# Two token tiles multiplied together, 512 columns wide, in a windowed-attention and two-layer kernel

## The chip, the cores and the metric

The kernel runs on one core of one Trainium2 chip. The metric is the device time of one execution in microseconds; the median of three runs before the change is 878.5 us (878.42 to 878.53).

## What is computed

Attention with a window of 128 keys and a linear position bias, then two feed-forward layers on its 2304 token rows (4 batches of 576, 8 heads of 64, so 512 features). Layer 1 is the one that the change works on.

```python
scores = scale * (q @ k.T) + slope * -abs(rel)      # masked to 0 <= rel < 128
x = softmax(scores) @ v                              # (2304, 512)
h = x @ moe_w_in;   g = h * clip(h + 3, 0, 6) / 6;   x = g @ moe_w_out        # 512 -> 2048 -> 512
h = x @ moe2_w_in;  g = s * relu(h)**2 + b;          out = g @ moe2_w_out
```

All weights come as float64 (two 32-bit words an element).

## The kernel before, in words

**Tiles.** Layer 1 cuts the 2304 token rows into eight tiles: tiles 0 to 3 have 256 rows (the first two query blocks of each batch), tiles 4 to 7 have 320. Its weights are 16 blocks of 128 hidden features; block `f` holds an input half (512 features by 128) and an output half (128 by 512). A `Step(t, f)` is one block for one tile: `h` (L939) multiplies 12 times into the one PSUM bank of tag `h`; `relu` (ScalarE, L950) reads that bank; `product` (VectorE, L953) reads it a last time and so frees it; `hi` (ScalarE, L960) and `lo` (VectorE, L964) split the result in two float32r parts; `o` (L977) multiplies 12 times into four accumulators. A number is split in a high and a low part everywhere, and three of the four products of parts are taken, hence 3 x 4 matmuls a group. After block 15, `end` (L990 to L995) scales the accumulators and stores the tile to DRAM.

**Weights.** Each float64 block is converted on the chip in two halves (`Half`, L319 on): `high` (ScalarE, L355) rescales the upper words into a staging buffer `staging_early`; a second ScalarE operation (L361) rescales the lower words; `sign` (VectorE, a shift L371 and an or L374, or one operation L366 for the halves in `SIGN_ON_POOL`, whose sign bit GpSimd has cut out at L358); `add` (GpSimd, L380); `hi` (ScalarE, L386); `lo` (VectorE, L390; GpSimd for four halves). All 32 halves are converted while tiles 0 and 1 are worked on.

**Order.** There is no scheduler at run time: each method is put in a numbered slot with a rank (`at`), a table `MOVED` shifts single ones, and the sorted list is the order in which every engine's queue is filled. A pair of slots is one `Step`. The first slots hold the attention of tile 0 and 1 (`StartUnit`) and warming matmuls (`FILLERS`). Steps of tile 0 come first; tile 1 follows three blocks behind (`LAG = 3`), alternating with tile 0. From tile 2 on a tile is done at a stretch, with the attention of the tile after it in between. A half's slots follow from its number:

```python
s = 4 * f + 2 * i if f > 4 else min(s - 6, 3 + 4 * f + 2 * i)
```

**Second layer.** Its weights are converted too (`Pair`, 16 of them, during tiles 2 to 7), written to DRAM through a staging buffer and the raw buffers (`target`, L1120), and read back as 1 MB chunks into a ring of five buffers (`Chunk`, L1161) when the second layer runs (L1410, L1344).

Of the kernel before, what the change touches and what calls it, by code (L numbers as in the profile page):

```python
# [12 lines left out]
I32 = mybir.dt.int32  # L13
# [13 lines left out]
COPIED_ON_VECTOR = ("0_0_2", "1_0_2", "1_0_6")  # L27

SIGN_ON_POOL = ("0_1", "4_0", "6_0")

HALF_SHIFTS = {
    "0_0": 2, "0_1": 1, "10_0": 1, "10_1": 1, "2_1": -1, "3_0": 1, "3_1": 1, "4_1": 2, "5_1": 1,
    "8_0": 1, "8_1": 1, "9_1": 1,
}

FILLERS = (3, 1, 0, 0, 0, 2, 2, 1, 2, 1, 0, 2, 0, 0)

KINDS = {"StartUnit": "S", "MidUnit": "M", "Unit": "U", "Step": "T", "Half": "H", "Pair": "P", "Rest": "R"}


def names(fn):
# [6 lines left out]
    if c is None:  # L48
        return ()
    m = method.__name__ + ("." + str(args[0]) if args else "")  # L50
    own = f"{o.t}_{o.f}" if c == "T" else str(o.i) if c == "P" else o.id
    kind = {
        "S": lambda: f"{o.g}{o.h % 2}", "M": lambda: o.h % 2, "U": lambda: o.h % 2, "R": lambda: "",
# [9 lines left out]
    "Ha0.load": (1, 0),  # L63
    "Ha1.high": (0, 2.05),
    "Ha1.lo": (0, -1.6),
# [21 lines left out]
    "S10.widen": (-1, 0),  # L87
# [24 lines left out]
    "M2_0_0.load_values": (2, 0),  # L112
    "M2_0_2.load_values": (-1, 0),
    "M2_0_3.to_lo": (-1, 0),
    "M2_0_4.exps": (-2, 0),
    "M2_0_5.weights": (2, 0.3),
    "M2_0_7.minima": (2, -1.92),
    "S01.to_lo": (1, -7.4),
# [8 lines left out]
    "S1_0_0.scale": (1, 0),  # L127
    "S1_0_2.exps": (1, -3.2),
# [11 lines left out]
    "T1_6.product": (0, -0.05),  # L140
}
# [3 lines left out]
def tile_alibi_window_attention_moe_moe2(  # L145
# [22 lines left out]
    N1 = max(SIZES1)  # L168
    N2 = 384
# [59 lines left out]
    own = const.tile([P, P], I32, name="own")  # L229
# [40 lines left out]
    def half_blocks():  # L270
        nonlocal own2, relp, slope
        own2 = ap.tile([P, HALF], I32, bufs=1, name="own2")
        relp = ap.tile([P, P], F32, bufs=1, name="relp")
        slope = ap.tile([P, H // 2], F32, bufs=1, name="slope")
        for i in (0, 1):
            p = slice(i * HALF, (i + 1) * HALF)
            nc.sync.dma_start(out=relp[p], in_=rel[:HALF])
            nc.sync.dma_start(out=own2[p], in_=own[:HALF, :HALF])
            for j in range(H // 2):
                nc.gpsimd.memset(slope[p, j : j + 1], slopes[2 * j + i])  # L280

# [36 lines left out]
    class Half:  # L318
# [29 lines left out]
        def high(self):  # L348


            if "early" not in late:
                late["early"] = ap.tile([P, 4 * DM], F32, tag="stage", bufs=1, name="staging_early")
# [559 lines left out]
    class Step:  # L912
# [17 lines left out]

        def h(self):
            w = wt[self.f]
            x = x_tile(self.t)
# [3 lines left out]
            for cc in range(CC):  # L937
                for wp, xp in ((0, 0), (0, 1), (1, 0)):
                    nc.tensor.matmul(  # L939
                        self.ps,  # L940
                        lhsT=w[:, wp, cc * P : (cc + 1) * P],
                        rhs=x[:, cc, xp],
# [5 lines left out]
        def relu(self):  # L948
            self.a = gpool.tile([P, N1], F32, tag="t", name=f"t{self.t}_{self.f}")[:, : self.n]
# [7 lines left out]
        def hi(self):  # L957
            self.g = gpool.tile([P, 2, N1], F32R, tag="g", name=f"g{self.t}_{self.f}")
# [6 lines left out]

        def o(self):
            t, f = self.t, self.f
            if f == 0:
                ids = ((0, 1), (2, 3))[t] if t < 2 else range(CC)
                acc[t] = [ps_o.tile([P, 512], F32, tag=f"o{d}", name=f"o{t}_{d}") for d in ids]  # L970
                if t < 2:
                    acc[t] = [a[:, i : i + 256] for a in acc[t] for i in (0, 256)]
                acc[t] = [a[:, : self.n] for a in acc[t]]
            w = wt[f]
            for i, (wp, gp) in enumerate(((0, 0), (1, 0), (0, 1))):
                for d in range(CC):
                    nc.tensor.matmul(  # L977
                        acc[t][d],
                        lhsT=w[:, wp, DM + d * P : DM + (d + 1) * P],
                        rhs=self.g[:, gp],  # L980
                        start=f == 0 and i == 0 and (t > 1 or d % 2 == 0),
# [3 lines left out]

        def end(self):
            t, n = self.t, self.n
            for e in range(0, CC, 2):
                y = gpool.tile([P, 2, N1], F32, tag="y", name=f"y{t}_{e}")[:, :, :n]
                nc.scalar.activation(y[:, 0], acc[t][e], AF.Copy, scale=1.0 / 6.0)  # L990
# [633 lines left out]
```

## Time and profile before

| | before |
|---|---|
| median of three runs | 878.5 us |
| the profiled execution, its own time | 878.33 us |
| its span, first to last instruction | 876.6 us |
| TensorE, VectorE, ScalarE, GpSimd busy | 99%, 72%, 59%, 39% of the span |
| mean granted TensorE clock | 0.998 of full speed |
| first `h` group; first `h` group of tile 2 | 29.24 us; 146.62 us |

TensorE's line shows when one of its instructions was in work; a row of the timeline gives start, length and, in brackets, the idle time before it with the instruction that ended it. Two rows that follow each other overlap a little, so the time that a group takes is read from one start to the next. In the shapes, `128x256` is partitions by columns.

### The profile page before, as it was taken

The numbers are of one execution on the slowest core, as the hardware profiler recorded it, in microseconds if no ns is written. First come the engines' busy times: TensorE is split into PE (matmuls) and PEld (weight loads), VectorE is DVE, ScalarE is ACT, GpSimd is POOL, SyncE is SP. The second block draws the span as 40 slices with busy tenths as digits, with TensorE's granted clock in tenths as the row PEclk, the third lists the DMA queues.
The fourth block names the chain that finished last, engine by engine and source line by source line (L and its number), as shares of the span: only waits on it lengthen the run. The fifth ranks groups of instructions, "written<-read, shape, count | busy, mean of one in ns | idle before, by whom it ended". The sixth has DMA issues, their size and how long they took to land.

```text
span 876.6 us, 17097 instructions
## 1 busy us (share of the span) xinstructions
PE 866.7 (99%) x6154; PEld 817.2 (93%) x6156; DVE 630.0 (72%) x1391; ACT 516.4 (59%) x1196; POOL 339.5 (39%) x539
## 2 busy tenths in 40 slices
PE   8999999999999999999999999999999999999998
PEld 5889899999999999999999999998899988999887
DVE  6898985566787677767657536779847789577784
ACT  7978875555665556465545436666356656366551
POOL 5644541334565454545534303453114450144200
PEclk9999999999999999999999999999999999999999
DMA  9554433526475556465555707887788787777873
GB/s 330 182 156 144 130 93 102 176 78 219 151 260 178 174 188 215 155 204 165 189 170 190 290 22 263 284 295 258 257 281 314 275 289 246 271 252 264 293 244 112
DMA packets 66821, 183.15 MB, mean 209 GB/s; under 512 B 9904, under 2 KB 29616, under 8 KB 58288
## 3 DMA queue, kind: packets, MB, share of 16 engines
q1 hardware_dynamic: 66736, 182.06, 61.4%
q8 instruction: 49, 0.80, 0.4%
q14 instruction: 36, 0.29, 0.1%
HBM read 143.13 MB, written 38.80 MB: 208 GB/s over the span
## 4 chain that ended last, share of the span: by engine, by line
PE 95%; DVE 3%; issue 1%; ACT 1%; ACTq 0%
PE h L939 23%; PE o L977 23%; PE h L1410 20%; PE o L1344 20%; PE v L687 2%; PE s L546 1%; PE t L643 1%; PE t L809 1%; PE tv L824 1%; PE v L888 1%; DVE w L390 1%; PE s L531 1%; PE s L778 1%; PE s L566 1%; PE warm_ps L224 1%
## 5 line engine op out<-in xcount | busy, mean ns | idle before, releaser
L977 PE MATMUL o<-g,w 128*128 128x256 f32 (+1 forms) x1536 | 233.0, 301 | 0.0
L939 PE MATMUL h<-x,w 128*128 128x256 f32 (+1 forms) x1536 | 227.8, 297 | 3.3 <-DVE t L953 3.3
L977 PEld LDWEIGHTS o<-g,w 128*128 128x128 f32 x1536 | 211.4, 190 | 7.5 <-issue 3.8
L939 PEld LDWEIGHTS h<-x,w 128*128 128x128 f32 x1536 | 211.9, 190 | 5.3 <-DVE t L953 4.3
L1410 PE MATMUL h<-x,wstream 128*128 128x384 f32 x1008 | 176.8, 334 | 0.0
L1344 PE MATMUL o<-wstream,i 128*128 128x256 f32 (+1 forms) x1032 | 176.4, 332 | 0.0
L1410 PEld LDWEIGHTS h<-x,wstream 128*128 128x128 f32 x1008 | 174.4, 188 | 0.8 <-ACT s L1420 0.6
L1344 PEld LDWEIGHTS o<-wstream,i 128*128 128x128 f32 x1032 | 155.3, 188 | 19.8
L950 ACT ACTIVATE t<-h 128x256 f32<-128x256 f32 (+1 forms) x128 | 52.4, 410 | 160.3 <-PE h L939 159.3
L953 DVE SCALAR_TENSOR_TENSOR t<-t,h 128x256 f32<-128x256 f32 (+1 forms) x128 | 57.7, 450 | 87.2 <-ACT t L950 86.7
L964 DVE TENSOR_TENSOR g<-t,g 128x256 fp32r<-128x256 f32 (+1 forms) x128 | 72.6, 567 | 19.4 <-ACT g L960 18.7
L1444 ACT ACTIVATE g<-g,scalar 128x384 f32<-128x384 f32 x96 | 58.5, 610 | 39.4 <-DVE g L1429 36.9
L1467 POOL TENSOR_TENSOR g<-g 128x384 f32<-128x384 f32 x24 | 24.3, 1012 | 112.3 <-PE h L1410 93.4
L960 ACT ACTIVATE g<-t 128x256 fp32r<-128x256 f32 (+1 forms) x128 | 56.2, 439 | 12.7 <-DVE t L953 12.5
L1428 DVE TENSOR_TENSOR g<-h,s 128x384 f32<-128x384 f32 x72 | 39.8, 552 | 31.3 <-PE h L1410 22.6
L672 POOL TENSOR_SCALAR_AFFINE_SELECT W<-F 128x128 f32<-128x128 f32 (+1 forms) x128 | 38.7, 337 | 33.5 <-ACT F L647 31.5
L622 POOL TENSOR_SCALAR P<-P,st 128x128 f32<-128x128 f32 x80 | 37.4, 481 | 32.0 <-DVE st L431 30.7
L1194 DVE SCALAR_TENSOR_TENSOR i<-g,scalar,i 128x768 fp32r<-128x768 f32 x48 | 49.2, 1071 | 0.6 <-ACT i L1193 0.6
L1429 DVE SCALAR_TENSOR_TENSOR g<-g 128x384 f32<-128x384 f32 x72 | 47.3, 658 | 2.5
L1091 POOL TENSOR_TENSOR work<-raw 128x512 int32<-128x512 int32 x28 | 29.9, 1086 | 39.7 <-ACT P L605 11.7
L1420 ACT ACTIVATE s<-h 128x384 f32<-128x384 f32 x72 | 34.7, 481 | 17.8 <-PE h L1410 17.4
L1193 ACT ACTIVATE i<-g,scalar 128x768 fp32r<-128x768 f32 x48 | 41.5, 930 | 5.8 <-PE o L1344 5.8
(147 smaller groups left out, 1175.0 us busy)
## 6 DMA issues: line engine op xcount, KB each, us to landing
wstream<-wo SPq DMA_DIRECT2D x42, 1024.0 KB, 4.9
raw<-w SPq DMA_DIRECT2D x53, 512.0 KB, 5.0
wstream<-wh SPq DMA_DIRECT2D x24, 1024.0 KB, 5.7
wstream<-wh SPq DMA_DIRECT2D x24, 768.0 KB, 6.0
wh<-staging_early SPq DMA_DIRECT2D x16, 512.0 KB, 3.6
wo<-staging_early SPq DMA_DIRECT2D x12, 512.0 KB, 3.2
stage<-w SPq DMA_DIRECT2D x11, 512.0 KB, 4.4
out<-u SPq DMA_DIRECT2D x11, 384.0 KB, 3.1
```

What stands on the lines that cost most here:

```text
L939: nc.tensor.matmul(self.ps, lhsT=w[:, wp, cc * P : (cc + 1) * P], rhs=x[:, cc, xp], start=m == 0, stop=m == 3 * CC - 1,)
L950: nc.scalar.activation(self.a, self.ps, AF.Relu, bias=3.0)
L953: nc.vector.scalar_tensor_tensor(out=self.a, in0=self.a, scalar=6.0, in1=self.ps, op0=ALU.min, op1=ALU.mult)
L960: nc.scalar.activation(self.g[:, 0], self.a, AF.Copy)
L964: nc.vector.tensor_tensor(out=self.g[:, 1], in0=self.a, in1=hi, op=ALU.subtract)
L977: nc.tensor.matmul(acc[t][d], lhsT=w[:, wp, DM + d * P : DM + (d + 1) * P], rhs=self.g[:, gp], start=f == 0 and i == 0 and (t > 1 or d % 2 ...
L1193: nc.scalar.activation(hi, src, AF.Identity, bias=b)
L1194: nc.vector.scalar_tensor_tensor(out=out[:, :, 1], in0=src, scalar=b, in1=hi.bitcast(F32), op0=ALU.add, op1=ALU.subtract,)
L1344: nc.tensor.matmul(self.acc[k][c][:, out], lhsT=g[:, gp, c * P : (c + 1) * P], rhs=w[:, cols], start=k in (0, 1, 5) and p == 0 and i == 0, ...
L1410: nc.tensor.matmul(self.ps[first], lhsT=w[:, wp, cc], rhs=x[:, cc, xp], start=n == first and m == 0, stop=m == 5, skip_group_check=True,)
L1429: nc.vector.scalar_tensor_tensor(out=g, in0=g, scalar=0.0, in1=g, op0=ALU.max, op1=ALU.mult)
L1444: nc.scalar.activation(g, g, AF.Copy, scale=s_sb)
```

## The change

From block 4 on the steps of tiles 0 and 1 are one (`Both`): one `h` group of 12 matmuls with 512 columns, one `relu`, `product`, `hi` and `lo` on 512 columns, one `o` group of 12 with 512 columns. The x of the two tiles lies in one buffer `both`; a wide `h` reads it as two runs of 256. The accumulators of the two tiles are now the halves of the same four banks. Blocks 0 to 3 stay at 256 columns and run first for tile 0, then for tile 1 (`LAG = 4`). The conversion of blocks from 5 on is planned six slots later (`LATER`), the steps that need them are as much later. `staging_early` is half as large (two places for `high` instead of four), the `Pair` stores come from other buffers, and the ring of chunks uses the two halves of `both`. Five `high` go from ScalarE to GpSimd (`HIGH_ON_POOL`), five more halves have their sign cut out on GpSimd (`SIGN_ON_POOL`), four copies of attention go from ScalarE to VectorE (`COPIED_ON_VECTOR`), three warming matmuls go, and `MOVED` has other entries.

```diff
-COPIED_ON_VECTOR = ("0_0_2", "1_0_2", "1_0_6")
+COPIED_ON_VECTOR = ("0_0_0", "0_0_2", "0_0_5", "0_0_7", "1_0_0", "1_0_2", "1_0_6")
+HIGH_ON_POOL = ("3_0", "4_1", "5_1", "6_0", "7_0")
-SIGN_ON_POOL = ("0_1", "4_0", "6_0")
+SIGN_ON_POOL = ("0_1", "10_0", "11_0", "1_1", "2_0", "4_0", "6_0", "8_1")
-FILLERS = (3, 1, 0, 0, 0, 2, 2, 1, 2, 1, 0, 2, 0, 0)
+FILLERS = (2, 1, 0, 0, 0, 1, 1, 1, 2, 1, 0, 2, 0, 0)
...
     "T0.h": (0, 9),
+    "T0.o": (0, 10.3),
...
-    LAG = 3
-    steps = []
-    for i in range(NF + LAG):
-        steps += [(0, i)] if i < NF else []
-        steps += [(1, i - LAG)] if i >= LAG else []
+    LAG = 4
+    steps = [(t, f) for t in range(2) for f in range(LAG)]
+    steps += [(t, f) for f in range(LAG, NF) for t in range(2)]
     steps += [(t, f) for t in range(2, nt1) for f in range(NF)]
...
+    for f in range(LAG, NF):
+        hslot[1, f] = hslot[0, f]
+        oslot[0, f] = oslot[1, f] = hslot[0, f] + (5 if f < NF - 1 else 3)
...
-        free = 4 if slot < FIRST else 2 if slot < hslot[1, 0] else 0
+        free = 4 if slot < FIRST + 2 else 0
...
-            self.zp = late["early"][:, late["z"] % 4 * DM :][:, :DM]
-            nc.scalar.activation(self.zp, self.h.bitcast(F32), AF.Copy, scale=2.0**-112)
+            self.zp = late["early"][:, late["z"] % 2 * DM :][:, :DM]
+            h = self.h.bitcast(F32)
+            if self.id in HIGH_ON_POOL:
+                nc.gpsimd.tensor_scalar(
+                    out=self.zp, in0=h, scalar1=2.0**-112, scalar2=1.0, op0=ALU.mult, op1=ALU.mult
+                )
+            else:
+                nc.scalar.activation(self.zp, h, AF.Copy, scale=2.0**-112)
...
+    both = xpool.tile([P, 2, 2 * CC * N1], F32R, name="both")
...
+    class Both(Step):
...
+        def plan(self):
+            s = hslot[0, self.f]
+            at(s + 1, 10, self.h)
+            at(s + 2, 30.05, self.relu)
+            at(s + 2, 31.5, self.product)
+            at(s + 3, 30.05, self.hi)
+            at(s + 3, 31.7, self.lo)
+            s = oslot[0, self.f]
+            at(s + 1, 10, self.o)
+            if self.f == NF - 1:
+                at(s + 1, 30, self.end)
...
+        def values(self, cc, xp):
+            return both[:, :, (2 * cc + xp) * N1A :][:, :, :N1A]
...
-            whole = staging(self.s) if j < 2 else self.raw.bitcast(F32)
-            return whole[:, j % 2 * 2 * DM : j % 2 * 2 * DM + n * DM]
+            if j < 2:
+                whole = self.raw.bitcast(F32)[:, j * 2 * DM :]
+            elif j == 2:
+                whole = staging(self.s)
+            else:
+                whole = self.L[:, self.kind * DM :]
+            return whole[:, : n * DM]
...
-    ring = ("s0", "s1", "x1", "x2", "s2")
+    ring = ("s0", "s1", 1, "x2", 0)
...
+    LATER = 6
...
-            s = 4 * f + 2 * i if f > 4 else min(s - 6, 3 + 4 * f + 2 * i)
+            s = 4 * f + 2 * i + LATER if f > 4 else min(s - 6, 3 + 4 * f + 2 * i)
...
-    ready = (done, done, done, done, max(done, half))
+    ready = (done, done, done, done, max(done, hslot[nt1 - 1, NF - 1] + 2))
```

Three places of the new order on which the prediction rests. In the names `t`, `h`, `o` and `g` are followed by tile and block or accumulator, `w1_5` is block 5 of the weights, and the last number is a buffer's.

VectorE before, from the `product` of tile 1's block 0 to that of tile 0's block 4:

```order
L953 SCALAR_TENSOR_TENSOR t1_0_779<-t1_0_779,h1_0_766 128x256
L371 TENSOR_SCALAR staging_early_246<-staging_early_246 128x512
L374 SCALAR_TENSOR_TENSOR raw1_206<-raw1_206,staging_early_246 128x512
L964 TENSOR_TENSOR g1_0_800<-t1_0_779,g1_0_800 128x256
L390 TENSOR_TENSOR w1_5_803<-raw1_206,w1_5_803 128x512
L371 TENSOR_SCALAR staging_early_246<-staging_early_246 128x512
L374 SCALAR_TENSOR_TENSOR raw0_205<-raw0_205,staging_early_246 128x512
L953 SCALAR_TENSOR_TENSOR t0_4_824<-t0_4_824,h0_4_811 128x256
```

VectorE in the changed kernel, from the `product` of tile 1's block 3 to the first wide one:

```order
L1001 SCALAR_TENSOR_TENSOR t1_3_878<-t1_3_878,h1_3_864 128x256
L432 TENSOR_TENSOR w1_4_764<-raw1_202,w1_4_764 128x512
L432 TENSOR_TENSOR w1_5_899<-raw1_202,w1_5_899 128x512
L413 TENSOR_SCALAR staging_early_241<-staging_early_241 128x512
L416 SCALAR_TENSOR_TENSOR raw0_201<-raw0_201,staging_early_241 128x512
L1012 TENSOR_TENSOR g1_3_896<-t1_3_878,g1_3_896 128x256
L408 SCALAR_TENSOR_TENSOR stage6_0_857<-staging_early_241,stage6_0_857 128x512
L1001 SCALAR_TENSOR_TENSOR t0_4_945<-t0_4_945,h0_4_907 128x512
```

Block 5's conversion stood right behind tile 1's first step; now it stands behind tile 1's fourth, before the first wide `product`.

TensorE before, around the `h` group of block 8 for tile 0:

```order
L977 MATMUL o0_0_607<-g0_7_1113,w1_7_985 128x256 x2
L977 MATMUL o0_1_608<-g0_7_1113,w1_7_985 128x256 x2
L939 MATMUL h0_8_1181<-x0_279,w1_8_1095 128x256 x12
L977 MATMUL o1_2_834<-g1_4_1170,w1_4_720 128x256 x2
L977 MATMUL o1_3_835<-g1_4_1170,w1_4_720 128x256 x2
```

TensorE in the changed kernel, around the wide `h` group of block 5:

```order
L987 MATMUL h0_5_956<-both_96,w1_5_899 128x512 x12
L1031 MATMUL o0_0_609<-g0_4_954,w1_4_764 128x512
L1031 MATMUL o0_1_610<-g0_4_954,w1_4_764 128x512
L1031 MATMUL o0_2_611<-g0_4_954,w1_4_764 128x512
L1031 MATMUL o0_3_612<-g0_4_954,w1_4_764 128x512
```

An `h` group and an `o` group of 256 columns for each tile, each weight loaded for both tiles in turn, became one of each with 512 columns.

ScalarE before, in the start, around the copies of two transposed units (`W0_0_4`, `W0_0_5`):

```order
L386 ACTIVATE w1_0_312<-raw1_206 128x512
L698 ACTIVATE x0_279<-tv0_0_3_297 128x256
L817 ACTIVATE W0_0_4_346<-t0_0_4_293 128x384
L817 ACTIVATE W0_0_5_350<-t0_0_5_334 128x384
L800 ACTIVATE P1_0_0_342<-P1_0_0_342,st_126 128x128
```

ScalarE in the changed kernel at the same place:

```order
L428 ACTIVATE w1_0_308<-raw1_202 128x512
L741 ACTIVATE both_96<-tv0_0_3_290 128x256
L860 ACTIVATE W0_0_4_343<-t0_0_4_319 128x384
L843 ACTIVATE P1_0_0_339<-P1_0_0_339,st_133 128x128
L843 ACTIVATE P1_0_0_339<-P1_0_0_339,st_133 128x256
```

The copy of unit 5 has left ScalarE for VectorE; three others of the start did the same.

## Rows read from the trace of the kernel before

**Rows 1.** The page's busy table: engine, busy us, share of the span, instructions.

```profile
PE 866.7 (99%) x6154; PEld 817.2 (93%) x6156; DVE 630.0 (72%) x1391; ACT 516.4 (59%) x1196; POOL 339.5 (39%) x539
```

**Rows 2.** Stretches: length, busy us by engine, granted clock, DMA share, GB/s.

```profile
12.00:28.00 16.00, 14.01 (x110) 10.98 (x112) 15.37 (x51) 15.72 (x37) 10.36 (x17) 1.00 0.94 361
...
52.00:56.00 4.00, 2.16 (x13) 1.96 (x12) 3.96 (x6) 3.05 (x6) 2.10 (x3) 0.81 0.75 223
56.00:60.00 4.00, 4.00 (x29) 4.00 (x29) 3.78 (x7) 2.95 (x6) 1.91 (x2) 0.77 0.44 142
60.00:120.00 60.00, 58.51 (x479) 54.37 (x478) 55.02 (x128) 51.09 (x129) 28.21 (x31) 1.00 0.46 139
120.00:870.00 750.00, 749.97 (x5244) 713.32 (x5243) 524.35 (x1111) 415.65 (x957) 277.60 (x436) 1.00 0.63 214
```

**Rows 3.** List of waits, TensorE: us in total, times, longest.

```profile
PE h L939 <- DVE t L953: 3.3, 4, 1.8
```

**Rows 4.** Timeline of VectorE before the longest gap: start, length.

```profile
50.92 1.53 DVE L390 TENSOR_TENSOR w<-raw,w 128x512 fp32r<-128x512 f32 x1
52.37 0.41 DVE L371 TENSOR_SCALAR staging_early<-staging_early 128x512 int32<-128x512 int32 x1
...
53.75 0.41 DVE L953 SCALAR_TENSOR_TENSOR t<-t,h 128x256 f32<-128x256 f32 x1
```

**Rows 5.** Timeline of TensorE behind that gap.

```profile
54.21 2.74 PE L939 MATMUL h<-x,w 128*128 128x256 f32 x12 [1.84 <-DVE t L953]
56.75 2.08 PE L977 MATMUL o<-g,w 128*128 128x256 f32 x12
58.67 1.60 PE L939 MATMUL h<-x,w 128*128 128x256 f32 x12
60.11 1.60 PE L977 MATMUL o<-g,w 128*128 128x256 f32 x12
...
63.05 0.93 PE L531 MATMUL s<-raw 64*128 64x128 f32 x8
63.91 1.70 PE L977 MATMUL o<-g,w 128*128 128x256 f32 x12
```

**Rows 6.** Timeline of TensorE, second layer; 512 and 256 columns alternate in L1344.

```profile
583.53 56.32 PE L1344 MATMUL o<-wstream,i 128*128 128x512 f32 x324
639.69 56.33 PE L1410 MATMUL h<-x,wstream 128*128 128x384 f32 x324
695.85 1.20 PE L1344 MATMUL o<-wstream,i 128*128 128x512 f32 x6
```

**Rows 7.** Timeline of VectorE, 61 to 64 us.

```profile
61.12 0.42 DVE L371 TENSOR_SCALAR staging_early<-staging_early 128x512 int32<-128x512 int32 x1
61.58 0.69 DVE L374 SCALAR_TENSOR_TENSOR stage<-stage,staging_early 128x512 int32<-128x512 int32 x1
62.19 0.42 DVE L964 TENSOR_TENSOR g<-t,g 128x256 fp32r<-128x256 f32 x1
62.52 1.53 DVE L390 TENSOR_TENSOR w<-stage,w 128x512 fp32r<-128x512 f32 x1
63.98 0.41 DVE L953 SCALAR_TENSOR_TENSOR t<-t,h 128x256 f32<-128x256 f32 x1
...
64.86 0.68 DVE L390 TENSOR_TENSOR w<-stage,w 128x512 fp32r<-128x512 f32 x1
```

**Rows 8.** Line L817, 8 to 40 us: ns min/median/max, first and last start.

```profile
L817 ACT ACTIVATE W<-t x13: 467/485/514, 9.8 to 39.2; 128x384 f32<-128x384 f32 x13
```

**Rows 9.** The page's DMA issues: count, KB each, median us to landing.

```profile
wstream<-wh SPq DMA_DIRECT2D x24, 1024.0 KB, 5.7
```

**Rows 10.** Line L358: ns min/median/max.

```profile
L358 POOL TENSOR_SCALAR raw<-raw x2: 669/670/672, 13.1 to 41.7; 128x512 f32<-128x512 f32 x2
```

**Rows 11.** Timeline of GpSimd at 62 us.

```profile
62.41 1.10 POOL L380 TENSOR_TENSOR stage<-stage 128x512 int32<-128x512 int32 x1 [1.96 <-DVE stage L374]
```

**Rows 12.** Groups by form, VectorE, 54 to 141 us: busy us, mean ns.

```profile
L390 DVE TENSOR_TENSOR w<-raw,w 128x512 fp32r<-128x512 f32 x15 | 15.8, 1051 | 1.2 <-ACT w L386 0.9
```

More of the change, by code (lines that the diff above doesn't have):

```diff
@@ L91 @@
     "S11.transposes": (-1, 2),
+    "S11.values": (0, -2),
     "T0.h": (0, 9),
+    "T0.o": (0, 10.3),
+    "T1.lo": (0, 6.3),
     "T1.o": (0, -1),
+    "T1.product": (0, -1.42),
+    "U0.scale": (1, 6.0),
     "H0_1.hi": (-1, 0),
+    "H11_0.high": (-2, 2.05),
+    "H13_0.load": (1, 0),
+    "H14_0.add": (0, 0.6),
     "H14_0.high": (-1, 0),
@@ L226, in tile_alibi_window_attention_moe_moe2 @@
     ident = const.tile([P, P], F32, name="ident")
-    own = const.tile([P, P], I32, name="own")
+    own = const.tile([P, P], I32, tag="own", name="own")
     rel = const.tile([P, P], F32, name="rel")
@@ L280, in half_blocks, with more_half_blocks @@
                 nc.gpsimd.memset(slope[p, j : j + 1], slopes[2 * j + i])
+    def more_half_blocks():
+        nonlocal relp
+        relp = const.tile([P, P], F32, tag="own", name="relp")
+        for i in (0, 1):
+            nc.sync.dma_start(out=relp[i * HALF : (i + 1) * HALF], in_=rel[:HALF])
     def scalars():
@@ L964, in lo, with banks @@
             nc.vector.tensor_tensor(out=self.g[:, 1], in0=self.a, in1=hi, op=ALU.subtract)
+        def banks(self):
+            t = self.t
+            if t == 1:
+                acc[1] = [a[:, N1A : 2 * N1A] for a in acc["both"]]
+                return
+            whole = [ps_o.tile([P, 512], F32, tag=f"o{d}", name=f"o{t}_{d}") for d in range(CC)]
+            acc[t] = [a[:, : self.n] for a in whole]
+            if t == 0:
+                acc["both"] = whole
         def o(self):
@@ L968, in o @@
             if f == 0:
[L969 to L973, printed above, removed]
+                self.banks()
             w = wt[f]
@@ L984, in o, with sums @@
                     )
+        def sums(self):
+            return acc[self.t]
         def end(self):
-            t, n = self.t, self.n
             for e in range(0, CC, 2):
-                y = gpool.tile([P, 2, N1], F32, tag="y", name=f"y{t}_{e}")[:, :, :n]
-                nc.scalar.activation(y[:, 0], acc[t][e], AF.Copy, scale=1.0 / 6.0)
+                ys, stores = self.places(e)
+                nc.scalar.activation(
+                    ys[0], self.split(self.sums()[e]), AF.Copy, scale=1.0 / 6.0
+                )
@@ L1008, in staging @@
         if k not in late:
-            pool, tag = (ap, "stage") if k == "early" else (xpool, "x1")
-            late[k] = pool.tile([P, 4 * DM], F32, tag=tag, bufs=1, name=f"staging_{k}")
+            if k == "early":
+                late[k] = ap.tile([P, 2 * DM], F32, tag="stage", bufs=1, name="staging_early")
+            else:
+                late[k] = both[:, 1, : 2 * DM].bitcast(F32)
         return late[k]
@@ L1163, in load @@
             if k not in streams:
-                pool = late["p"] if ring[k] == "s2" else xpool
-                streams[k] = pool.tile([P, 4 * DM], F32, tag=ring[k], bufs=1, name=f"wstream{k}")
+                if ring[k] in (0, 1):
+                    streams[k] = both[:, ring[k], : 4 * DM].bitcast(F32)
+                else:
+                    streams[k] = xpool.tile([P, 4 * DM], F32, tag=ring[k], bufs=1, name=f"wstream{k}")
             n = self.src.shape[1]
@@ L1486, in tile_alibi_window_attention_moe_moe2 @@
     first = hslot[3, 0] + 3
-    starts = [76, 96] + [first + 10 * i for i in range(2 * NP - EARLY)]
+    starts = [74 + LATER, 97] + [first + 10 * i for i in range(2 * NP - EARLY)]
     for i, s in enumerate(starts):
@@ L1498, in tile_alibi_window_attention_moe_moe2 @@
             at(-3 if u.g == 0 else 4 + u.h // 2, 1, u.load)
-    for tf in steps:
-        Step(*tf).plan()
+    for t, f in steps:
+        if t > 1 or f < LAG:
+            Step(t, f).plan()
+        elif t == 0:
+            Both(f).plan()
     base = FIRST + 2 * len(steps) + 1
```

114 lines of the change are left out of this document (79 added, 35 removed).

## The prediction

> **What bounds the kernel now.** I first read the page's busy table: TensorE works for 99% of the span [rows 1]. Stretch by stretch the reader then sees where the missing 1% lies [rows 2]: from 120 us on TensorE has no gap (749.97 of 750 us); between 12 and 28 us it idles 2.0 of 16 us while ScalarE (15.72) and VectorE (15.37) are full; between 52 and 60 us it idles 1.84 us and its granted clock falls to 0.81 and 0.77; between 60 and 120 us it idles 1.5 of 60 us, beside a VectorE that is busy for 55.0. So the change can act in two ways: it makes TensorE's own work shorter, or it takes away gaps in the first 120 us. What TensorE does after that is untouched, and whatever is gained or lost before it shifts the end by as much.
>
> The list of waits gives the gaps one name: all four gaps in front of an `h` group after 40 us, 3.3 us together, end with VectorE's `product` [rows 3]. There is one PSUM bank of tag `h`; the next `h` group may not write it before the `product` of the last step has read it. The longest case can be followed on VectorE [rows 4]: it takes up the `lo` of block 5 at 50.92 (1.53 us), then a shift and an or of yet another half, and only at 53.75 the `product`; `h` of tile 1 starts at 54.21 [rows 5]. After this gap the clock is low: the `h` group takes 54.21 to 56.75, the `o` group 56.75 to 58.67, that is 2.54 and 1.92 us where the next group needs 1.44 (58.67 to 60.11) [rows 5].
>
> **Term 1, wider matmuls.** From block 4 on, 12 blocks x 24 pairs = 288 pairs of 256 columns become 288 matmuls of 512. A group of twelve at 256 columns steps by 1.44 us, 120 ns each [rows 5]. The trace has 512 columns only in the second layer, alternating with 256: 324 instructions, 162 pairs, from 583.53 to 639.69, 346.7 ns a pair [rows 6]; less 120 this leaves 226.7 ns. The 384-column stretch behind it (324 in 56.16 us, 173.3 ns) lies on the same line: 0.4167 ns a column, which is the 2.4 GHz level, and 13.3 ns per matmul whatever its width. So a pair falls from 240 to 226.7 ns: 288 x 13.3 ns = **3.8 us**. The Trainium skill, "TensorE: Matmul & The Clock Gate", section "Back-to-back issue gap", puts what an isolated matmul takes beyond its columns at about 2.5 ns, and says that in a stream the weight loads help set the spacing. By the 2.5 ns this term would be 0.7 us; the rows disagree, and I go by them. What no row shows: the right operand of a wide `h` is read as two runs of 256, since the two tiles lie apart in `both`. If each run paid the 13.3 ns again, the `h` half would give nothing: lower bound 1.9 us.
>
> **Term 2, the gap at 52.4 us.** In the old order five conversion operations and a step's `lo` stand between the `product` of tile 1's block 0 and that of tile 0's block 4, because block 5 is wanted two steps later; in the new order all four steps of tile 1 pass first, and between the products of its blocks 0 and 1 there is only one `lo` of the step and one of weights. The gap (1.84 us) and the slow stretch (1.10 + 0.48 us) go: **3.4 us**. What is late next is the `product` of block 4: before it stand two `lo` of weights, shift, or, the step's `lo` and a sign operation. By steps [rows 7] shift 0.46, or 0.61, step's `lo` 0.33; a `lo` of weights 0.61 when free (0.68 long, 0.07 of it under the next) and 1.46 when blocked (62.52 to 63.98); the sign operation I put at 0.61 to 1.1. That is 3.2 to 5.4 us, with the `product` itself (0.61 at 512 columns) 3.8 to 6.0. TensorE meanwhile has the wide `h` (12 x 226.7 ns = 2.7), scores (0.86, 63.05 to 63.91 [rows 5]) and one `o` group of 1.44: 5.0 us. New wait 0 to 1.0, I take 0.4, the middle.
>
> **Term 3, the other three gaps** (3.3 less 1.84 = 1.5 us). They came from one VectorE operation too many in front of a `product`, with one `o` group of 1.44 us as cover. A wide `o` group covers 2.7 us; relu and `product` themselves grow less than that, to some 0.65 and 0.61 us (ScalarE's 384-column copy takes 0.49 [rows 8]). VectorE's load hardly changes: 55.0 of 60 us are busy [rows 2]; product and `lo` of a block cost 4 x 0.33 now and 2 x 0.61 then, and the three shifts that go to GpSimd after block 7 give back 3 x 0.46. Some 92% stays 92%, so I let half of the gaps go, **0.75 us**, and book 0.4 for new ones.
>
> **Term 4, the start.** Four copies go from ScalarE to VectorE (0.49 each [rows 8], 1.9 us), block 3's first `high` to GpSimd; two shifts leave VectorE (0.46 each). Both engines are full from 12 to 28 us [rows 2], and TensorE's 2.0 us of idle time there is the most that can come back; VectorE is loaded by 1.0 us more, and the attention units get three PSUM banks where they had five for the last steps before tile 1, so up to 1.5 us may be lost. I take 0.
>
> **Edits booked at nothing.** The merged `end` copies two banks on each of ScalarE and VectorE, 512 columns, about 0.65 each, 1.3 us; before `o` of tile 2 needs the banks TensorE has two `h` groups and scores, 3.7 us. Eight stores of 128 KB take the place of four of 256 KB; nothing on TensorE waits for them. Staging for `high` has two places instead of four: a `high` now waits for the sign of two halves before, which in the new order stands ahead of the last `product` on VectorE. The fifth stream of the second layer's weights now lands where tile 7 lay, so it starts after tile 7's last `h`; its first use is twelve groups of six 384-column matmuls later, 12.5 us, against 5.7 to land [rows 9]. Without that cover TensorE would stop for the rest.
>
> **Sum.** -3.8 - 3.4 - 0.75 + 0.8 = -7.2 us. The profiled execution took 878.33 us (span 876.6, 1.7 around it), 0.2 below the median of 878.5; 878.5 - 7.2 gives **871.3 us**.
>
> **Rivals.** *The waits stay, only in other places* (VectorE is as full as before, which speaks for it; the doubled cover speaks against): term 1 alone counts, 1.9 to 3.8 us, so 874.7 to 876.6; I put it at 875.5.
>
> *The width brings nothing* (two runs cost two matmuls, or the spacing has another cause than a cost per matmul): the change does not do what it says, and terms 2 and 3 remain, 3.4 us: 875.1. The straight line through three widths speaks against it; the strided operand, which no row shows, for it.
>
> *Slower: VectorE sets the pace.* The place is the wait of each wide `h` for the `product` before it. Ten operations go to GpSimd, 0.67 us each [rows 10], and GpSimd's work stops VectorE's two-input operations: the `lo` of weights that starts at 62.52, inside an add of GpSimd (62.41, 1.10 us [rows 11]), takes 1.53 us and not 0.68 [rows 7]; the mean is 1.05 [rows 12]. If all 24 `lo` of weights in these blocks were blocked (1.46 for a mean of about 0.97) and all 12 of the steps by 0.85 as well, VectorE would need 12 + 10 = 22 us more. Its slack is 8% of some 80 us, 6.5; the remaining 15.5 us would be waits of TensorE: 878.5 - 7.2 + 15.5 = 886.8, and from 13.7 us of extra blocking on the kernel is slower than now. Against it: the moved operations last 7 us in all, and not all meet a `lo`. The Trainium skill, "SBUF — State Buffer", section "Who interferes with whom", calls the ports that the two engines share an exclusive lock; the trace agrees with its one long row. By that rule each microsecond moved to GpSimd can cost VectorE at most as much, 7 us, which the slack almost holds.
>
> **How the numbers follow.** Forecast 0.62; waits stay 0.17; width brings nothing 0.09; VectorE sets the pace 0.12, two thirds of it past the point where the kernel is slower. The best sum I can defend is -3.8 - 4.9 - 2.0 = -10.7 (867.8); the low end of the range leaves a little of that out, the high end takes in the two middle rivals: **868.8 to 876.3**. A measurement of this kernel tells 0.2% (1.8 us) from no change. Faster by more than that 0.87: the forecast, nearly all of the two middle rivals and a little of the last; within it 0.05; slower 0.08.
>
> **What would show it.** Right: `h` and `o` groups of 512 columns that step by 2.7 us per twelve; no gap above 0.5 us in front of an `h` group after 40 us, clock 1.00 in every stretch; tile 2's first `h` some 7 us before its present place; from there on every group as far apart as now. Wrong: groups of 2.9 us (width), gaps in front of wide `h` groups released by `product` (waits), GpSimd rows of 0.7 us beside `lo` rows of 1.5 us throughout (pace), or a first `h` of tile 0 that moves by more than 1.5 us (start).

## The result, and the profile after

The changed kernel takes 870.68 us (median of 4 runs, 869.64 to 871.59) against 878.48 (878.42 to 878.53): ratio 0.9911, 95% interval 0.9894 to 0.9928. The forecast was 871.3, the range 868.8 to 876.3. The profiled execution took 871.4 us with a span of 869.7, where before had 876.6.

The page's busy table of the changed kernel (columns as in [rows 1]):

```profile
PE 861.5 (99%) x5865; PEld 798.1 (92%) x5865; DVE 619.3 (71%) x1364; ACT 510.6 (59%) x1161; POOL 353.0 (41%) x549
```

TensorE has 289 matmuls less in its records, yet only 5.2 us less busy time; GpSimd has 13.5 us more. The stretches of the same execution (columns as in [rows 2]):

```profile
12.00:28.00 16.00, 14.32 (x102) 10.50 (x102) 13.92 (x50) 13.07 (x31) 11.28 (x18) 0.89 0.90 329
52.00:56.00 4.00, 4.00 (x36) 4.00 (x35) 2.78 (x7) 2.76 (x6) 0.83 (x1) 1.00 0.02 6
56.00:60.00 4.00, 4.00 (x34) 3.96 (x33) 2.81 (x6) 2.09 (x5) 2.67 (x4) 1.00 0.00 0
60.00:120.00 60.00, 59.86 (x304) 45.62 (x304) 55.44 (x121) 52.95 (x121) 38.99 (x40) 1.00 0.52 161
120.00:860.00 740.00, 739.97 (x5087) 700.01 (x5086) 519.56 (x1092) 415.05 (x944) 280.73 (x435) 1.00 0.64 217
```

Between 52 and 60 us TensorE is now full, at a granted clock of 1.00; before it idled 1.84 us there and had 0.81 and 0.77 [rows 2]. Between 60 and 120 us it idles 0.14 us, before 1.49, beside a VectorE that is as busy as ever (55.4 of 60 against 55.0). Only the start is worse here: a clock of 0.89 between 12 and 28 us.

TensorE's waits, all that the view lists (us in total, times, longest):

```profile
PE tv L867 <- DVE W L858: 1.7, 2, 1.1
PE s L821 <- POOL raw L803: 1.4, 1, 1.4
PE warm_ps L256 <- DVE warm L251: 1.3, 1, 1.3
PE tv L867 <- ACT W L860: 0.5, 1, 0.5
```

The row `h <- product` of [rows 3] is gone; all that is left lies in the start. TensorE's timeline: the row of the start that takes too long, the first `h`, the first three wide `h` groups (blocks 4 to 6), and the first `h` of tile 2:

```profile
17.45 1.48 PE L821 MATMUL s<-raw 64*128 64x128 f32 x8
...
30.95 1.66 PE L987 MATMUL h<-both,w 128*128 128x256 f32 x12
...
59.59 2.96 PE L987 MATMUL h<-both,w 128*128 128x512 f32 x12
62.48 0.93 PE L574 MATMUL s<-raw 64*128 64x128 f32 x8
63.33 1.69 PE L1031 MATMUL o<-g,w 128*128 128x256 f32 x12
65.16 3.06 PE L987 MATMUL h<-both,w 128*128 128x512 f32 x12
68.06 2.89 PE L1031 MATMUL o<-g,w 128*128 128x512 f32 x12
70.78 2.96 PE L987 MATMUL h<-both,w 128*128 128x512 f32 x12
...
141.61 1.58 PE L987 MATMUL h<-x,w 128*128 128x256 f32 x12
```

From one start to the next the wide `h` takes 2.90 us and the wide `o` 2.72. Eight matmuls of scores at 17.45 us take 1.48 us, where such a row takes 0.93 elsewhere: between 18 and 21 us the granted clock is 0.50. The first `h` comes at 30.95 us, 1.7 later than before (29.24).

For the experiments I use two marks that every kernel here has, since the work up to each is the same in all: the start of the first `h` group and of the first one with 320 columns (tile 4), at 29.24 and 261.28 us before, at 30.95 and 254.53 in the changed kernel. From the second mark to the last matmul the two differ by under 0.1 us. So the 6.9 us of span are **+1.7 us in the start and -8.5 us in the middle** (232.04 to 223.58 us), and 0.1 at the end.

| kernel | median us | ratio to before, interval | first `h` | middle |
|---|---|---|---|---|
| before | 877.8 to 878.5 | | 29.24 | 232.0 |
| changed | 870.68 | 0.9911 (0.9894 to 0.9928) | 30.95 | 223.6 |
| again (the same) | 870.36 | 0.9910 (0.9897 to 0.9924) | 29.16 | 223.6 |
| split256 | 871.82 | 0.9931 (0.9916 to 0.9945) | 29.46 | 225.4 |
| split256h | 870.74 | 0.9919 (0.9905 to 0.9934) | 29.16 | 224.1 |
| onerun | 869.93 | 0.9909 (0.9892 to 0.9925) | 29.60 | 223.6 |
| h_by_part | 870.04 | 0.9907 (0.9893 to 0.9922) | 29.23 | 223.8 |
| conv_early | 881.00 | 1.0031 (1.0017 to 1.0045) | 29.47 | 235.9 |
| h5_later | 879.29 | 1.0014 (1.0005 to 1.0023) | 28.95 | 233.1 |
| block5_later | 879.65 | 1.0021 (1.0012 to 1.0031) | 29.17 | 233.3 |
| high_on_pool | 877.97 | 1.0000 (0.9991 to 1.0009) | 29.42 | 231.7 |
| pool_before | 872.15 | 0.9930 (0.9916 to 0.9945) | 30.65 | 225.1 |
| fillers | 869.85 | 0.9905 (0.9892 to 0.9919) | 29.31 | 223.7 |
| start_before | 870.02 | 0.9906 (0.9891 to 0.9921) | 29.51 | 223.6 |

### The profile page after: what moved, and what is told of

It is laid out like the page before. It is cut to its first block, busy times and chain, and to the rows that moved or that the text cites. A ratio compares the mean times of both kernels' runs of the same rounds, so it can differ in the third digit from the quotient of the medians.

```text
span 869.7 us, 16435 instructions
## 1 busy us (share of the span) xinstructions
PE 861.5 (99%) x5865; PEld 798.1 (92%) x5865; DVE 619.3 (71%) x1364; ACT 510.6 (59%) x1161; POOL 353.0 (41%) x549
## 4 chain that ended last, share of the span: by engine, by line
PE 96%; DMA 1%; DVE 1%; issue 0%; SPq 0%; ACT 0%; POOL 0%; ACTq 0%; POOLq 0%
PE o L1031 24%; PE h L987 23%; PE h L1521 20%; PE o L1455 20%; PE v L730 2%; PE s L589 1%; PE t L686 1%; PE tv L867 1%; PE t L852 1%; DMA raw<-qk 1%; PE v L931 1%; PE s L574 1%; PE s L609 1%; DMA raw<-qkv0p 1%; PE s L821 0%
## 5 line engine op out<-in xcount | busy, mean ns | idle before, releaser
L1031 PE MATMUL o<-g,w 128*128 128x320 f32 (+2 forms) x1392 | 228.7, 314 | 0.0
L987 PE MATMUL h<-both,w 128*128 128x320 f32 (+2 forms) x1200 | 197.8, 314 | 0.1
L987 PEld LDWEIGHTS h<-both,w 128*128 128x128 f32 x1200 | 177.2, 188 | 6.7 <-DVE t L1001 0.5
L1521 PEld LDWEIGHTS h<-x,wstream 128*128 128x128 f32 x612 | 106.4, 188 | 0.8 <-ACT s L1531 0.6
L1455 PE MATMUL o<-wstream,i 128*128 128x512 f32 (+1 forms) x588 | 104.2, 333 | 0.0
L1455 PEld LDWEIGHTS o<-wstream,i 128*128 128x128 f32 x588 | 89.2, 188 | 11.1
L1455 PE MATMUL o<-both,i 128*128 128x256 f32 (+1 forms) x444 | 78.3, 332 | 0.0
L1012 DVE TENSOR_TENSOR g<-t,g 128x320 fp32r<-128x320 f32 (+2 forms) x116 | 66.0, 569 | 16.0 <-ACT g L1008 15.2
L1521 PE MATMUL h<-x,both 128*128 128x384 f32 x396 | 76.4, 334 | 0.0
L1455 PEld LDWEIGHTS o<-both,i 128*128 128x128 f32 x444 | 66.7, 188 | 8.5
L1521 PEld LDWEIGHTS h<-x,both 128*128 128x128 f32 x396 | 69.3, 188 | 0.0
```

What stands on the lines that cost most here:

```text
L987: nc.tensor.matmul(self.split(self.ps), lhsT=w[:, wp, cc * P : (cc + 1) * P], rhs=self.values(cc, xp), start=m == 0, stop=m == 3 * CC - 1,)
L1012: nc.vector.tensor_tensor(out=self.g[:, 1], in0=self.a, in1=hi, op=ALU.subtract)
L1031: nc.tensor.matmul(self.sums()[d], lhsT=w[:, wp, DM + d * P : DM + (d + 1) * P], rhs=self.g[:, gp], start=f == 0 and i == 0 and t != 1, st ...
L1455: nc.tensor.matmul(self.acc[k][c][:, out], lhsT=g[:, gp, c * P : (c + 1) * P], rhs=w[:, cols], start=k in (0, 1, 5) and p == 0 and i == 0, ...
L1521: nc.tensor.matmul(self.ps[first], lhsT=w[:, wp, cc], rhs=x[:, cc, xp], start=n == first and m == 0, stop=m == 5, skip_group_check=True,)
```

## Experiments

### Is it the width? split256, split256h

```diff
- nc.tensor.matmul(
-     self.split(self.ps),
-     rhs=self.values(cc, xp),
+ for t in (0, 1):
+     nc.tensor.matmul(
+         self.ps[:, t * N1A : (t + 1) * N1A],
+         rhs=x_tile(t)[:, cc, xp],
```

The same in `o` (not in split256h).

> The changed kernel with its order, conversion plan and buffers, but every matmul of 512 columns as two of 256 columns with the same weights (first tile 0, then tile 1): 288 matmuls more, the columns the same. From the first h group to the first h group of 320 columns the changed kernel takes 223.6 us (30.95 to 254.53). If the width's gain is a cost per matmul of 13.3 ns, as my prediction has it: 3.6 to 3.8 us more there, 227.3, and the whole at about 874.4. If the order alone did it and the width brings nothing: 223.6 and 870.7. If a second matmul with the same weights is cheaper than one with new ones: in between.

> As the run before, but only the wide h groups are cut in two (144 matmuls more); the wide o groups stay at 512. Equal cost per matmul in both: 1.8 us more than the changed kernel between the first h group and the first one of 320 columns, 225.4 us. If the right operand in two runs of 256 already costs the wide h part of this (its matmuls step by 233 ns, those of o by 228), cutting it costs less: 144 x (240 - 233) = 1.0 us, 224.6. If two runs cost as much as two matmuls: 223.6, no change.

TensorE's timeline of split256, whose groups are now 24 matmuls of 256 columns, and below it the row of the second mark:

```profile
63.66 3.10 PE L1087 MATMUL h<-both,w 128*128 128x256 f32 x24
66.60 3.03 PE L1109 MATMUL o<-g,w 128*128 128x256 f32 x24
69.47 3.00 PE L1087 MATMUL h<-both,w 128*128 128x256 f32 x24
...
254.86 1.34 PE L987 MATMUL h<-both,w 128*128 128x320 f32 x8
```

The `h` group takes 2.94 us (2.90 when wide), the `o` group 2.87 (2.72). The middle grows by 1.8 us, not by 3.6: 0.5 us of it in `h` (split256h against the changed kernel) and 1.3 in `o`. So the width of the matmuls is worth 1.8 us, the rest of the change 6.6 us (232.0 to 225.4); split256 keeps the wide `relu`, `product`, `hi` and `lo`, which belong to that rest.

### Why a wide `h` steps longer than a wide `o`: onerun, h_by_part

```diff
+ pair = flat[:, : 4 * CC * N1A].rearrange("p (c h t n) -> p c h t n", c=CC, h=2, t=2)
- return both[:, :, (2 * cc + xp) * N1A :][:, :, :N1A]
+ return pair[:, cc, xp]
```

> The changed kernel with the x of tiles 0 and 1 laid side by side for each part, so that a wide h reads 512 columns in one run (the attention that writes x writes the same shapes to other places). If the two runs cost the 5 ns by which a wide h steps longer than a wide o: its matmuls step by 228 ns, 144 x 5 ns = 0.7 us less, 222.9 us between the first h and the first one of 320 columns, the whole 0.7 us below the changed kernel. If the 5 ns come from something else (the bank it writes, the engine that reads it): 233 ns and no change. Lower bound of my prediction, 13.3 ns for each run: 227 - 13 is out of reach, since it steps by 233 already.

```diff
- for cc in range(CC):
-     for wp, xp in ((0, 0), (0, 1), (1, 0)):
+ for wp, xp in ((0, 0), (1, 0), (0, 1)):
+     for cc in range(CC):
```

> The changed kernel with the 12 matmuls of every h group of layer 1 in the order of o: all four feature blocks of one product of parts, then of the next, so that the two matmuls that use the same high part of a weight no longer follow each other. If that sequence is what makes a wide h step by 233 ns where a wide o steps by 228: 144 x 5 ns = 0.7 us less in the middle, 222.9. If the 5 ns have another cause (one bank for all twelve, where o goes round four): 223.6.

Neither changes the middle (223.6 and 223.8), and the wide `h` matmuls keep a median of 233 to 234 ns from start to start. Neither the two runs of the right operand nor the sequence of the weights shows a cost. One bank for all twelve, against `o`'s four in turn, is what is left of my guesses; it wasn't tried.

### Is it the order of the conversion? conv_early, h5_later, block5_later

```diff
- LATER = 6
+ LATER = 0
```

> The changed kernel with the conversion of blocks 5 to 15 planned six slots earlier, as before (LATER = 0): shift, or and lo of block 5 and 6 stand again between the products of the steps at 256 columns of tile 1. If the late plan took away the gap at 52 us: between two products VectorE then has 2.6 to 4.3 us of work where TensorE has two groups of 1.44, so gaps of 0.5 to 1.5 us come back in front of the h groups between 47 and 62 us, 1.5 to 4 us with what the clock loses behind them; the whole at 872.5 to 875. If the gap went because tile 1's steps no longer alternate with tile 0's, and the plan does not matter: 870.7, no gap above 0.3 us.

881.0 us: without the late plan the new order is slower than the kernel before. The edit moves a little more than the expectation says: the first `Pair` of the second layer's weights is planned six slots earlier too, and the other entries of the tables, made for the late plan, stay. TensorE's timeline where it begins to wait, and the stretches of 52 to 60 and 60 to 120 us:

```profile
48.10 1.12 PE L1031 MATMUL o<-g,w 128*128 128x256 f32 x8
50.30 0.74 PE L1031 MATMUL o<-g,w 128*128 128x256 f32 x4 [1.08 <-DVE g L1012]
50.88 1.58 PE L987 MATMUL h<-both,w 128*128 128x256 f32 x12
52.30 1.12 PE L1031 MATMUL o<-g,w 128*128 128x256 f32 x8
54.84 0.74 PE L1031 MATMUL o<-g,w 128*128 128x256 f32 x4 [1.43 <-DVE g L1012]
56.62 2.64 PE L987 MATMUL h<-both,w 128*128 128x256 f32 x12 [1.03 <-DVE t L1001]
...
91.77 1.54 PE L931 MATMUL v<-W,rv 128*64 128x256 f32 x6 [1.39 <-ACT W L939]
```

```profile
52.00:60.00 8.00, 5.54 (x33) 5.13 (x33) 7.56 (x11) 4.24 (x9) 5.37 (x6) 0.81 0.46 153
60.00:120.00 60.00, 57.03 (x282) 43.88 (x282) 50.76 (x108) 48.35 (x110) 32.25 (x33) 0.94 0.43 139
```

The gaps that I expected are there (3.5 us between 50 and 57), but they end mostly with the step's `lo` (L1012), which the last third of an `o` group waits for, and only once with `product`. What I had not expected is the rest: the attention that runs beside the wide steps gets late too (2.6 us of waits for `W`), and the granted clock falls twice, at 0.81 and 0.94 in these stretches. The middle grows by 12.3 us.

Can the old order have the same for a smaller edit?

```diff
- "8_0": 1, "8_1": 1, "9_1": 1,
+ "5_0": 2, "8_0": 1, "8_1": 1, "9_1": 1,
```

That is h5_later, in the table `HALF_SHIFTS` of the kernel before; block5_later, in the line above it:

```diff
- "0_0": 2, "0_1": 1, "10_0": 1, "10_1": 1, "2_1": -1, "3_0": 1, "3_1": 1, "4_1": 2, "5_1": 1,
+ "0_0": 2, "0_1": 1, "10_0": 1, "10_1": 1, "2_1": -1, "3_0": 1, "3_1": 1, "4_1": 2, "5_0": 2, "5_1": 3,
```

> The kernel before, with only the first half of block 5 converted two slots later (its shift, or and lo leave the stretch between the product of tile 1's block 0 and that of tile 0's block 4; what else stood there stays). If VectorE's operations in front of that product are the cause of the 1.84 us gap and of the slow clock behind it, as the second term has it: five operations, 2.5 us, in place of seven with a lo of 1.46; the gap falls to 0.5 us or less, the clock stays at 1.00, and the whole is 2 to 3.4 us below before (middle stretch 228.6 to 230 instead of 232.0). If it only moves to the next product (block 5 is then late for its own h, which comes two steps on): no change, 232.

> The kernel before, with both halves of block 5 converted two slots later. This time I counted the rows of the order: between the product of tile 1's block 0 and that of tile 0's block 4 stand two pairs of shift and or and the step's lo, 2.5 us; but in front of the next product (tile 1's block 1) stand a sign operation, two lo of weights, the step's lo and another pair, 1.4 + 1.0 + 0.3 + 1.1 + 1.1 = 4.9 us, where TensorE has two groups, 2.9 us. If it is the amount of VectorE's work in a step of the old order that makes the gap: it moves to the h group behind that product, 1.5 to 2 us long, and the whole stays within 1 us of before. If only the place in front of the product of block 4 was bad: 875 to 876.

h5_later failed as an experiment: I had counted wrongly what the shift of two slots leaves in front of the product. Three pairs of shift and or stand there instead of two, and the gap is the same 1.82 us. Nor do they keep their usual lengths: beside GpSimd's operations three of these rows take 1.45, 1.26 and 1.01 us where such rows take 0.69, 0.42 and 0.69 elsewhere, which is 1.9 us more. In block5_later the place is cleared, and the gap moves on. TensorE's timeline:

```profile
52.98 1.58 PE L939 MATMUL h<-x,w 128*128 128x256 f32 x12
54.47 1.54 PE L977 MATMUL o<-g,w 128*128 128x256 f32 x8
56.44 0.74 PE L977 MATMUL o<-g,w 128*128 128x256 f32 x4 [0.44 <-DVE g L964]
58.44 1.70 PE L939 MATMUL h<-x,w 128*128 128x256 f32 x12 [1.26 <-DVE t L953]
...
70.01 1.69 PE L939 MATMUL h<-x,w 128*128 128x256 f32 x12 [1.03 <-DVE t L953]
```

The `h` that had waited 1.84 us starts at 52.98 without a wait; the next one waits 1.26, one behind it 1.03. The whole is 1.4 us above before. That VectorE simply has too much to do in these steps, as my expectation had it, is not shown: before the `product` that the `h` at 58.44 waits for, VectorE itself stands still for 1.24 us until GpSimd has cut out a sign:

```profile
53.91 0.69 DVE L366 SCALAR_TENSOR_TENSOR stage<-staging_early,stage 128x512 int32<-128x512 int32 x1 [1.24 <-POOL stage L358]
```

### The operations moved to GpSimd: high_on_pool, pool_before

```diff
- HIGH_ON_POOL = ("3_0", "4_1", "5_1", "6_0", "7_0")
+ HIGH_ON_POOL = ("3_0", "4_1") + tuple(f"{f}_{i}" for f in range(5, 16) for i in (0, 1))
```

> The changed kernel with the high of all halves of blocks 5 to 15 on GpSimd: 19 more operations of 0.66 to 0.88 us, 13 to 17 us, taken off ScalarE. This tries my third rival, that GpSimd's work stops VectorE. GpSimd is busy 39 of 60 us between 60 and 120, VectorE 55.4. If each microsecond on GpSimd stops VectorE for as long: 13 us and more against a slack of 8% of 80 us, 6.4: at least 6 us slower, 877, with gaps in front of wide h groups ended by product. If only what happens to lie beside a two-input operation counts, as the mean lo of weights suggests (738 ns in the changed kernel, 1051 before, although GpSimd was busier): 0 to 2 us, 870.5 to 872.5.

878.0 us, 7.6 above the same kernel without the edit (again, 870.36). The price is that of my third rival, the mechanism for the most part is not. VectorE's waits, the row that "again" does not have, then TensorE's:

```profile
DVE staging_early L413 <- POOL staging_early L393: 8.9, 7, 2.0
```

```profile
PE h L987 <- DVE t L1001: 2.5, 3, 1.9
PE v L931 <- ACT W L939: 2.3, 1, 2.3
...
PE t L852 <- DVE x L745: 1.0, 1, 1.0
PE t L852 <- DVE st L905: 0.7, 1, 0.7
```

These four are 6.5 of the 8.1 us by which the middle is longer. VectorE's shift waits 8.9 us for `high`, which stands in GpSimd's queue behind adds and the weights of attention; the `product` behind it on VectorE is late with it. VectorE's own rows grow less: in the stretch 59 to 141 us the mean `lo` of weights from a raw buffer is 823 ns against 736 in "again" (1.3 us over 15 of them), the step's `lo` 876 against 747 (1.4 us over 11). That is a third of the 8.1 us.

```diff
- HIGH_ON_POOL = ("3_0", "4_1", "5_1", "6_0", "7_0")
+ HIGH_ON_POOL = ()
- SIGN_ON_POOL = ("0_1", "10_0", "11_0", "1_1", "2_0", "4_0", "6_0", "8_1")
+ SIGN_ON_POOL = ("0_1", "4_0", "6_0")
```

> The changed kernel with the five high back on ScalarE and the five more signs back on VectorE (each one operation with a sign cut out on GpSimd becomes a shift and an or). VectorE gets 5 more shifts of 0.46 us, three of them behind 59 us, where it is busy 55.4 of 60 us; ScalarE 5 x 0.65 us. By my third term, which moved them at next to nothing: 0 to 1 us slower, 870.4 to 871.4. If the moved operations are what keeps VectorE ahead of the products: gaps in front of wide h groups come back, 2 us and more, 872.5 or above. If GpSimd was the burden: faster.

1.8 us slower than "again"; 1.5 of it in the middle. TensorE's waits that come back:

```profile
PE h L987 <- DVE t L1001: 0.5, 1, 0.5
PE o L1031 <- DVE g L1012: 0.2, 1, 0.2
```

The four runs (871.83 to 872.68) lie wholly above the five of "again". Of the 1.5 us, 0.4 lie in the first `h` group itself, which takes 1.99 us to the next start where "again" needs 1.60; the operations moved in the start may be behind that part. So the few operations that the change moves to GpSimd pay, and nineteen more cost four times as much.

### The start: again, fillers, start_before

> The changed kernel as it is, once more, to see how its runs spread: four runs gave 869.6, 870.0, 871.4 and 871.6. The profiled one (871.4) has its granted clock at half for 3.4 us from 17.7 us on and its first h at 30.95 us, where three variants that differ only behind 59 us have no such dip and the first h at 29.2 to 29.6. If the dip is what splits the runs, they fall in two groups 1.7 us apart, 869.8 and 871.5; if the spread is something else, they fill the range.

```diff
- FILLERS = (2, 1, 0, 0, 0, 1, 1, 1, 2, 1, 0, 2, 0, 0)
+ FILLERS = (3, 1, 0, 0, 0, 2, 2, 1, 2, 1, 0, 2, 0, 0)
```

> The changed kernel with the warming matmuls of before (three more, at 5 to 6 us and at 9 to 14 us; 0.22 us each). If TensorE's idle time in the start, which the three leave open, is what lets the clock fall in some runs: no dip in any run, all at 869.5 to 870. If the dip hangs on when the first loads land (the second scores wait for raw until 6.9 to 7.2 us) the fillers change little: two groups as before. In both cases the middle (first h to first h of 320 columns) stays at 223.6 us.

start_before has this and the copies of before:

```diff
- COPIED_ON_VECTOR = ("0_0_0", "0_0_2", "0_0_5", "0_0_7", "1_0_0", "1_0_2", "1_0_6")
+ COPIED_ON_VECTOR = ("0_0_2", "1_0_2", "1_0_6")
```

> The changed kernel with the warming matmuls and the copies of before (four copies of 0.49 us back from VectorE to ScalarE), that is the fourth term undone, order apart. If the moved copies are worth nothing, as I booked them: first h at 29.2 to 29.6, the whole within 1 us of the changed kernel. If ScalarE's full 12 to 28 us (15.7 of 16 before, 14.6 in the changed kernel without the dip) is what they relieve: up to 4 x 0.49 = 2 us later. The middle stays at 223.6.

The five runs of "again" lie at 869.70, 869.85, 870.36, 870.47 and 871.13: by their times alone they fill the range. By the mean granted clock that is on record for each run they do fall in two groups. Of the nine runs of the changed kernel three have 0.998 (871.13, 871.40 and 871.59 us), six have 0.999 or 1.000 (869.64 to 870.47): 1.5 us between the medians, near the 1.7 of the profiled dip. Only one of the three was profiled, so where the clock fell in the other two is not known. The profiled run of "again", in stretches and with its first `h`:

```profile
12.00:28.00 16.00, 13.98 (x112) 10.71 (x113) 15.21 (x55) 14.51 (x34) 12.89 (x21) 1.00 0.93 339
```

```profile
29.16 1.66 PE L987 MATMUL h<-both,w 128*128 128x256 f32 x12
```

TensorE idles more here between 12 and 28 us (2.0 us against 1.7), at a clock of 1.00, and the first `h` is 1.8 us earlier. With the fillers of before the median is 869.85, with the copies too 870.02 (four runs within 0.3 us); the intervals overlap all over. All eight of these runs have a mean clock of 1.000, but so have the 16 runs of split256, split256h, onerun and h_by_part, which have the fillers and copies of the changed kernel. No part of the start's edits can be told from nothing, and why the clock fell in one profiled run stays open. For the same reason no variant here can be said to beat the changed kernel.

## Why the prediction held, step by step

The time came out 0.6 us from the forecast, but that is partly luck: errors cancelled in it. The forecast took 7.2 us off. In the profiles the middle is 8.5 us shorter: the width gave 2.0 us less than I said, the other gaps, the new waits and what stands in no term 3.3 us more. The start costs nothing or 1.7.

- **Term 1, width: 3.8 us said, 1.8 measured.** The mechanism is right, the size was not. The step that failed is "so a pair falls from 240 to 226.7 ns". 226.7 came from the second layer and holds for a wide `o` (median 228 ns), but a wide `h` steps by 233, and a group of twelve takes 2.90 us, which is my own sign that the width was wrong; the `o` group's 2.72 is the sign that it was right. And the two halves with the same weights step by 117 to 120 in `h`, not by 120 throughout. I had seen the doubt, "if each run paid the 13.3 ns again", and its bound of 1.9 us is what came; yet its reason is refuted by onerun, so the bound was met by luck. The Trainium skill, "TensorE: Matmul & The Clock Gate", section "Back-to-back issue gap", gives 2.5 ns beyond the columns for an isolated matmul and says that in a stream the weight load and the matmul set the spacing together; by the 2.5 ns an estimate of this term would be 0.7 us, and the measured 1.8 lies between that and the rows.
- **Term 2, the gap at 52.4 us: 3.4 us said, and 3.4 gone in the profile.** Idle time and slow clock are both gone there. In the times the slow clock counts for less than its 1.6 us. Of the 42 runs of the kernel before that stand beside the experiments, 18 have a mean granted clock of 1.000 (median 877.84 us) and 20 have 0.998, the profiled run's value (878.60): 0.8 us apart. And in h5_later, where the clock stayed at 1.00 behind the same gap, TensorE then waited 0.45, 0.20 and 0.19 us, and the middle was 1.0 us longer than before. So part of what the slow clock took may only stand in the place of waits. The new wait of 0 to 1.0 us in front of block 5's wide `h` (0.4 taken) is too short for the profile to list as idle: in "again" that `h` starts 1.81 us after the `o` group before it, where such a group behind scores needs 1.53 (block5_later, 64.36 to 65.89 us). The sign operation in front of block 4's `product`, which I put at 0.61 to 1.1 us, took 1.45 in the changed kernel (62.98 to 64.43 us). conv_early shows that the new order needs the late plan; the two smaller edits found no room in the old order, but they were only two places.
- **Term 3, the other gaps: 0.75 less 0.4 said, 1.4 measured.** "I let half of the gaps go" was too careful: all went (1.49 us of idle time between 60 and 120 us became 0.14). And the moved GpSimd operations, which I counted as three shifts, are worth 1.5 us in the middle (pool_before). Why all went is not settled. In the kernel before, the `product` that ends each of these three gaps stands right behind a `lo` of weights of 1.53 us, and each of these runs beside an add of GpSimd. VectorE's timeline of the kernel before, then GpSimd's:

```profile
66.86 1.53 DVE L390 TENSOR_TENSOR w<-stage,w 128x512 fp32r<-128x512 f32 x1
...
95.00 1.53 DVE L390 TENSOR_TENSOR w<-stage,w 128x512 fp32r<-128x512 f32 x1
...
99.06 1.53 DVE L390 TENSOR_TENSOR w<-raw,w 128x512 fp32r<-128x512 f32 x1
```

```profile
66.74 1.10 POOL L380 TENSOR_TENSOR stage<-stage 128x512 int32<-128x512 int32 x1 [3.23 <-DVE stage L374]
...
94.77 1.20 POOL L380 TENSOR_TENSOR raw<-raw 128x512 int32<-128x512 int32 x1
...
98.94 1.10 POOL L380 TENSOR_TENSOR raw<-raw 128x512 int32<-128x512 int32 x1 [2.97 <-DVE raw L374]
```

The 0.85 us above a free `lo` (0.68) are more than any of the three gaps (0.29, 0.59 and 0.61 us). In the changed kernel the mean `lo` from a raw buffer between 54 and 141 us is 738 ns, before 1051 [rows 12]. So the gaps can have gone because the wide groups cover more, as I argued, or because a `lo` meets an add less often in the new order; no run here separates the two.

- **Not in any term: 1.9 us** (8.5 less 1.8, 1.84, 1.6 and 1.4). Counted from the starts in the trace, twelve steps from one matmul of 256 columns to the next last 138 to 279 ns in the kernel before (listed idle time taken off, the slow stretch left out), and three in split256: 0.9 us, which I take for waits too short to show as idle. Most of the rest is half a nanosecond in each of some 1400 matmuls; no run tells its cause.
- **Term 4, the start: 0, right where the clock stays up** (first `h` at 29.16 to 29.60 us in seven profiles that have the start of the changed kernel, 29.24 before); 1.7 us late in the one where it fell, just past the bound of 1.5. The first `h` of tile 2 came 5.0 us earlier in that profile and 6.7 in "again" (139.88), where I had said some 7; one more `o` group of tile 1 now stands ahead of it.
- **Edits booked at nothing** stayed so: from the first 320 columns on nothing differs, and neither the staging, nor the merged end, nor the fifth stream shows in TensorE's waits.
- **Rivals.** "The waits stay" is false for the change and true for both smaller edits of the old order. "The width brings nothing" is false too, though the width brought only half of what I said. "VectorE sets the pace" can be brought about (high_on_pool) at about the price that I gave, through waiting in GpSimd's queue. The Trainium skill, "SBUF — State Buffer", section "Who interferes with whom", calls the shared ports an exclusive lock; by that, GpSimd's extra work would lengthen VectorE's rows, and these grew by 2.7 us in the two kinds of `lo`, where VectorE waited 8.9 us in a queue's order.

## What to carry to other kernels

A gap that ends with one late operation was not closed here by moving that operation's neighbours, in two tries. Before trying, count what the engine has to do between two such points in the order, with the lengths that the rows have there and not at their shortest, and what it waits for itself; compare that with the work that the engine which bounds the kernel has in the same stretch. Take a price per instruction from the same kind of group, since the same width stepped at 228 ns in one and 233 in the other. And before moving work to an idle engine, look at who waits for its result and what stands before it in that engine's queue.

## What was not expected of the hardware

The same gap can cost the clock or not: 1.84 us at 52.4 us lowered it in the kernel before (0.81 and 0.77 granted), 1.82 us at the same place in h5_later did not (its `h` behind the gap takes 1.53 us, start to start, not 2.54). In the start, 1.7 us of idle time came with a clock of 0.89 and 2.0 us with 1.00. The runs of one kernel differ too: of 42 runs of the kernel before, 18 have a mean granted clock of 1.000 and 20 have 0.998. So the 1.6 us that the slow clock took in term 2 belong to that one execution, and not to every gap of that length.
